# A Fourier mixing and maxout kernel: other load order, full-array transposes and engine orders in batch 0

## Chip, cores, metric

One core of a Trainium2 chip. The metric is device time of one launch in microseconds (us). "Span" is the part of it that the trace covers, some 2 us less. All runs told here are of state fast.

In the views of the profile, PE is TensorE, PEld its weight loads, DVE is VectorE, ACT ScalarE, POOL GpSimd; PEclk is the granted TensorE clock as a share of the full one. A line of the waits view says who waited for whom, then us in total, times, longest us. A timeline line gives start and length in us and ends in the idle time before it and what ended that. A "look" is the traced run of a kernel in a job; a "job" is a set of kernels run in turns on one chip.

## The reference, cut to what matters

```python
X = np.fft.rfft(x, axis=1)                       # x: (8, 3072, 256)
y = np.fft.irfft(X * (filt_r + 1j * filt_i), n=3072, axis=1)
h1 = y @ w1;  h2 = y @ w2                        # 24576 tokens, 256 -> 1024
out = np.maximum(h1, h2) @ w_out                 # -> 256
```

The kernel splits 3072 as 128 x 24 and does the transforms as matmuls. max(h1, h2) is taken as relu(h1 - h2) + h2, so Wd = w1 - w2, and M = w2 @ w_out.

## The kernel before, as far as it matters

Batch 0 is worked off first, in SBUF alone; the others go through DRAM (f1, f2) beside the dense part (s4, moe_h, moe_o), which fills TensorE. In batch 0: S1 (128-point transform), T1 (transposes), s2 (24-point, with the sine table U), pq (product with the filter, which is expanded into F), s3 (inverse, with the tables VP and VQ; ScalarE copies its result to Zt), T2 (transposes), then s4. F_r is the filter's real part as loaded. For the later batches f1 writes ad in DRAM, bt is what is read back of it, and s2 of f2 reads bt.

```python
for c in range(6): load_x(0, c)                  # in front of the iotas, on GpSimd's queue
load_f(0); load_f(1)
G.iota(pid, ...)                                 # five more follow; C1, the cosine table, needs them
...
def first_t1(g, E):                              # 16 transposes of half the array
    for c, i, dh, b in ...:                      # [loops joined]
        TE.transpose(pt[64*b:64*b+64, c, i, 128*dh:128*dh+128], a_[:, 2*(t0+4*c+i) + b], I128)

def first_s2(g, pool):                           # [s2's matmuls into px cut]
    for k in range(2):
        pq.append(pqpool.tile([128, 2, 2, D], BF16, tag="pq", name="pq"))
        E, src = V, px[:, k]
        if k == 1 and pool:                      # one of the two products on GpSimd,
            E = G                                # which needs ScalarE's copy xs
            src = apool.tile([128, 2, D], FP32, tag="at", name="xs")
            S.activation(src[0:FROWS], px[0:FROWS, k], AF.Copy)
        E.tensor_tensor(pq[k][0:FROWS], src..., F[0:FROWS, :, k, 2*g:2*g+2], OP.mult)
...
for n, g in enumerate(order):                    # the product loop, eight groups
    if n < 7: expand_f(order[n + 1], 1, S)       # filter rows to F: 16 matmuls, a ScalarE copy
    if n == 6: fix_f()
    pq = first_s2(g, n in (0, 2, 4))
    if n in (1, 3, 5): prep_wd(n // 2, *wf)      # w2 as bf16, Wd: on GpSimd
    if pend: first_s3(*pend)                     # s3 of the group before
    pend = g, pq
```

## Time and profile before

| | before |
|---|---|
| time | 563.4 us, median of 2 (562.47 to 564.33) |
| first pq / last Zt copied | 34.2 / 61.1 us |
| first s4 / copy of M begins (the first moe_o follows) | 63.0 / 82.8 us |
| from M (start of its copy, here and below) to the end | 478.4 us |

The table follows the chain in time: up to the first pq the filter and U must be ready; to the last Zt runs the product loop; to M the first tiles and the weight preparation; the rest is dense. The lines are in the prediction.

### The profile page before, as it was taken

Reading aid. Unit: us, or ns where it says so; the run is one execution under the profiler, and the core shown is the slowest. Engines: PE = TensorE matmul, PEld = TensorE weight load, DVE = VectorE, ACT = ScalarE, POOL = GpSimd, SP = SyncE. Lnnn points to the kernel's source line nnn. Section 1 sums busy time; section 2 is a strip of 40 time slices with the busy share of each in tenths; the row PEclk is TensorE's granted clock in tenths of the full one; section 3 lists DMA queues with packets and bytes.
Section 4 is the critical chain, followed back from the end, with each engine's and each line's share of the span. In section 5 each row is a group of like instructions: output and inputs, shape, how many; then the busy total and the mean of one; then the engine's idle time right before and its main releaser. Section 6 shows DMA issues by size and latency. Waiting matters only on the chain.

```text
span 561.2 us, 12527 instructions
## 1 busy us (share of the span) xinstructions
PE 513.0 (91%) x5324; PEld 355.3 (63%) x5401; DVE 317.1 (57%) x420; ACT 341.3 (61%) x601; POOL 70.3 (13%) x123
## 2 busy tenths in 40 slices
PE   2866689999999999999999999998999999999992
PEld 2743446666766766667666666676666666677771
DVE  5746414963586357634874387545873578434430
ACT  4576474776578657775677557754776456555440
POOL 7127001101100120011100210012000000000000
PEclk9875689999999999999999999999999999999997
DMA  9950258568967894669856994689566926421111
GB/s 171 282 95 11 49 138 133 129 166 262 181 143 234 212 228 124 189 175 217 191 125 198 214 216 117 200 203 209 127 182 167 196 97 163 123 75 76 67 48 75
DMA packets 67596, 87.07 MB, mean 155 GB/s; under 512 B 3986, under 2 KB 48276, under 8 KB 66452
## 3 DMA queue, kind: packets, MB, share of 16 engines
q1 hardware_dynamic: 51908, 44.31, 36.3%
q0 software_dynamic: 15632, 41.95, 28.2%
q8 instruction: 42, 0.69, 0.5%
q14 instruction: 14, 0.11, 0.1%
HBM read 53.74 MB, written 47.19 MB: 180 GB/s over the span
## 4 chain that ended last, share of the span: by engine, by line
PE 48%; issue 18%; DMA 5%; DVE 2%; POOL 1%; ACT 0%; POOLq 0%; SPq 0%
PE po L527 18%; PE ph L502 16%; PE po L522 4%; DMA bt<-ad 3%; PE pz L372 3%; PE px L391 3%; PE pa L337 2%; PE py L486 2%; DMA ad<-at 2%; DVE pq L396 1%; POOL out_dram L533 1%; ACT at L338 0%; SPq L347 0%; DVE ot L529 0%; DVE gt L505 0%
## 5 line engine op out<-in xcount | busy, mean ns | idle before, releaser
L507 ACT ACTIVATE gt<-ph 128x512 bf16<-128x512 f32 x307 | 182.8, 602 | 114.5 <-PE ph L502 113.6
L527 PE MATMUL po<-Wo,gt 128*128 128x256 bf16 x1536 | 229.8, 273 | 3.2
L527 PEld LDWEIGHTS <-gt 128*128 128x128 bf16 x1536 | 150.3, 98 | 57.5
L396 DVE TENSOR_TENSOR pq<-px,F 120x1024 bf16<-120x1024 f32 x112 | 131.6, 1217 | 24.0 <-PE px L391 23.2
L529 DVE COPY ot<-po 128x512 f32<-128x512 f32 x96 | 66.2, 690 | 110.6 <-PE po L527 110.0
L376 ACT ACTIVATE zt<-pz 112x512 bf16<-112x512 f32 x112 | 60.8, 594 | 45.9 <-PE pz L372 40.6
L502 PEld LDWEIGHTS <-Wd 128*128 128x128 bf16 x768 | 70.3, 98 | 26.2 <-issue 12.4
L533 POOL DMA_DIRECT2D out_dram<-ot x48 | 25.8, 537 | 453.5 <-DVE ot L529 415.3
L505 DVE TENSOR_SCALAR gt<-ph 128x512 bf16<-128x512 f32 x77 | 52.8, 686 | 35.1 <-PE ph L502 27.5
L338 ACT ACTIVATE at<-pa 128x512 bf16<-128x512 f32 x84 | 50.4, 615 | 7.7 <-PE pa L337 6.2
L337 PE MATMUL pa<-xb,C 128*128 128x512 bf16 x83 | 31.2, 383 | 0.6 <-ACT zr L434 0.5
L486 PE MATMUL py<-G,zr 128*128 128x128 bf16 x384 | 30.2, 221 | 1.5 <-DVE zr L432 0.8
L372 PE MATMUL pz<-pq,VP 56*64 56x256 bf16 x448 | 28.7, 271 | 1.0 <-DVE pq L396 0.8
L486 PEld LDWEIGHTS <-zr 128*128 128x128 bf16 x384 | 25.1, 99 | 6.8 <-issue 3.5
L372 PE MATMUL pz<-pq,VQ 56*64 56x256 bf16 x448 | 28.0, 268 | 0.0
L92 POOL DMA_DIRECT2D xb<-in_x_dram x48 | 26.2, 556 | 9.9 <-DMA Fs<-in_filt_i_dram 3.9
L391 PE MATMUL px<-bt,U 48*64 48x256 bf16 x448 | 23.7, 281 | 1.6 <-DMA bt<-ad 1.6
L451 DVE TENSOR_TENSOR pq<-px,F 120x1024 bf16<-120x1024 f32 x13 | 15.2, 1215 | 11.1 <-PE px L441 5.2
L391 PEld LDWEIGHTS <-U 48*64 48x64 bf16 x448 | 8.3, 104 | 13.8 <-issue 11.8
L434 ACT ACTIVATE F<-pf 128x1024 bf16<-128x1024 f32 x16 | 15.5, 1031 | 1.7 <-PE pf L115 1.7
L464 PE MATMUL pz<-VP,pq 56*128 56x48 bf16 x128 | 6.9, 213 | 10.2 <-POOL pq L451 6.1
L372 PEld LDWEIGHTS <-VP 56*64 56x64 bf16 x448 | 13.2, 106 | 3.1 <-DVE pq L396 1.6
(354 smaller groups left out, 562.9 us busy)
## 6 DMA issues: line engine op xcount, KB each, us to landing
out_dram<-ot POOLq DMA_DIRECT2D x48, 512.0 KB, 4.5
xb<-in_x_dram POOLq DMA_DIRECT2D x48, 256.0 KB, 7.3
ad<-at SPq DMA_DIRECT2D x42, 256.0 KB
bt<-ad SPq DMA_DIRECT2D x28, 384.0 KB
zd<-zt SPq DMA_DIRECT2D x56, 192.0 KB
zr<-zd SPq DMA_DIRECT2D x14, 768.0 KB
wf<-in_moe_w_dram POOLq DMA_DIRECT2D x2, 1024.0 KB, 16.5
Fs<-in_filt_r_dram POOLq DMA_DIRECT2D x1, 768.0 KB, 11.6
```

What stands on the lines that cost most here:

```text
L337: TE.matmul(pa, C1, xb[b, c // 2][:, 2 * (c % 2):2 * (c % 2) + 2], start=True, stop=True)
L338: S.activation(at[:, 2 * (c % 2):2 * (c % 2) + 2], pa, AF.Copy)
L372: TE.matmul(pz[c][64 * k:64 * k + 64, i], W[64 * c:64 * c + 56, 2 * g + i, k], pq[k][64 * c:64 * c + 56, ri, i], start=(ri == 0), stop=(ri ...
L376: S.activation(zt[0:ROWS, c, o:o + 2], pz[c][0:ROWS], AF.Copy)
L391: TE.matmul(px[k][64 * c:64 * c + 64, i], U[64 * k:64 * k + 48, t_], bt_[64 * k:64 * k + 48, t_], start=True, stop=True)
L396: V.tensor_tensor(pq[k][0:FROWS], px[k][0:FROWS].rearrange("p (o i) d -> p o i d", o=1).to_broadcast([FROWS, 2, 2, D]), F[0:FROWS, :, k, 2 ...
L486: TE.matmul(py[:, n], zr[b][:, 4 * i + n, 128 * dc:128 * dc + 128], G1, start=True, stop=True)
L502: TE.matmul(ph, Wd[:, dc, 128 * j:128 * j + 128], y_[:, dc].rearrange("p a b -> p (a b)"), start=(dc == 0), stop=(dc == 1))
L505: V.tensor_scalar(gt[tt][:, j], ph, 0.0, None, OP.max)
L507: S.activation(gt[tt][:, j], ph, AF.Relu)
L527: TE.matmul(p_, g_[:, jj, 128 * n:128 * n + 128], Wo[:, jj], start=False, stop=(jj == 7))
L529: V.tensor_copy(ot[tt][:, n - 1:n + 1], po[tt])
```

## The change

The intent is to shorten the stretch in which TensorE isn't the bound: tables at once, ScalarE occupied with the filter while x is still landing, full-array transposes, a product loop that doesn't wait on GpSimd, a warm TensorE, and ScalarE relieved in the first tiles. The core of the diff (cuts marked with ...):

```diff
-    for c in range(6):
-        load_x(0, c)
-    load_f(0)
-    load_f(1)
     pid = init.tile([128, 1], FP32)
 ... iotas ...
+    load_f(0)
+    load_x(0, 0)
+    load_x(0, 1)
 ... Sel, two loads of x0, I128 and SW, two loads ...
+    load_f(1)
-    def spin(n):
-        pd = p2.tile([128, 2, 512], FP32, tag="p2", name="pd")
+    def spin(pd, n):
 ...
-            S.activation(w2T[:, 2 * jp:2 * jp + 2], pt, AF.Copy)
+            V.tensor_copy(w2T[:, 4 * k:4 * k + 4], pt)        # bf16 transposes, in two parts
 ...
-        S.activation(at[:, 2 * (c % 2):2 * (c % 2) + 2], pa, AF.Copy)
+        evac(V if b == 1 and c % 2 else S, at[:, 2 * (c % 2):2 * (c % 2) + 2], pa)
 ...
-                          C1.rearrange("p (k a) -> p a k", a=2), start=True, stop=True)
+                          C1.rearrange("p (t b a) -> p b a t", b=2, a=2), start=True, stop=True)
 ...
-                    for b in range(2):
-                        TE.transpose(pt[64 * b:64 * b + 64, c, i, 128 * dh:128 * dh + 128],
-                                     a_[:, 2 * (t0 + 4 * c + i) + b], I128)
+                    TE.transpose(pt[:, c, i, 128 * dh:128 * dh + 128],
+                                 At[:, 2 * dh:2 * dh + 2].rearrange("p b m t -> p t (b m)")[:, t0 + 4 * c + i], I128)
 ...
+        if pool:
+            xs = apool.tile([128, 2, D], FP32, tag="at", name="xs")
+            S.activation(xs[0:FROWS], px[0:FROWS, 1], AF.Copy)
         pq = []
 ...
         pz = p2.tile([128, 2, 512], FP32, tag="p2", name="pz")
+        spin(pz[:, 0], 2)
 ...
+    order = (1, 0, 2, 3, 4, 5, 6, 7)
+    for e, c in ((3, 0), (1, 1), (0, 2), (1, 3), (0, 4), (0, 5)):
+        for _ in range(e):
+            expand_f(order[len(done)], 0, S)
+            done.append(0)
         first_s1(c)
 ...
     for n, g in enumerate(order):
 ...
-        if n < 7:
-            expand_f(order[n + 1], 1, S)
 ...
-        pq = first_s2(g, n in (0, 2, 4))
+        pend.append(first_s2(g, n in (2, 4, 6)))
 ...
-        if pend:
-            first_s3(*pend)
-        pend = g, pq
-    first_s3(*pend)
 ...
+        if n < 6:
+            expand_f(order[n + 2], 1, S)
+        if n > 1:
+            first_s3(*pend.pop(0))
+    first_s3(*pend.pop(0))
+    first_s3(*pend.pop(0))
 ...
-        plan(j - 1, first_t2, j, (S, V)[j % 2], ps)
-    plan(7, prep_w)
+        plan(j - 1, first_t2, j, V, ps)
+    plan(4, prep_w, 0)
+    plan(5, prep_w, 1)
+    plan(6, prep_w, 2)
-    plan_f2(1, spaced(19, 1.8, 9), 29, 35)
+    plan_f2(1, spaced(18, 1.8, 9), 28, 34)
```

The two matmuls of `spin` write where s3 writes next, and nothing reads them.

More of the change, by code (lines that the diff above doesn't have):

```diff
@@ L72 @@
     xpool = ctx.enter_context(tc.tile_pool(name="xpool", bufs=8))
-    apool = ctx.enter_context(tc.tile_pool(name="apool", bufs=6))
+    apool = ctx.enter_context(tc.tile_pool(name="apool", bufs=5))
     bpool = ctx.enter_context(tc.tile_pool(name="bpool", bufs=2))
@@ L156 @@
            allow_small_or_imprecise_dtypes=True)
+    load_f(0)
+    load_x(0, 0)
+    load_x(0, 1)
     V.memset(I128, 0.0)
+    V.memset(Sel, 0.0)
     V.memset(SW, 0.0)
-    V.memset(Sel, 0.0)
-    V.memset(U.rearrange("p t (q x) -> p t q x", q=2)[:, :, :, 24:32], 0.0)
-    V.memset(VP[:, :, :, 48:64], 0.0)
+    sl = Sel[:, :, 0:24].rearrange("p m (q j) -> p m q j", q=2)
+    for q in range(2):
+        G.affine_select(out=sl[:, :, q], in_=sl[:, :, q], pattern=[[-1, 8], [-8, J]], compare_op=OP.not_equal,
+                        fill=1.0, base=0, channel_multiplier=1)
+    load_x(0, 2)
+    load_x(0, 3)
     G.affine_select(out=I128, in_=I128, pattern=[[-1, 128]], compare_op=OP.not_equal,
@@ L167 @@
                         fill=1.0 - 2.0 * q, base=-12 * (1 - q), channel_multiplier=1)
-    sl = Sel[:, :, 0:24].rearrange("p m (q j) -> p m q j", q=2)
-    for q in range(2):
-        G.affine_select(out=sl[:, :, q], in_=sl[:, :, q], pattern=[[-1, 8], [-8, J]], compare_op=OP.not_equal,
-                        fill=1.0, base=0, channel_multiplier=1)
+    load_x(0, 4)
+    load_x(0, 5)
+    load_f(1)
     def table_c():
@@ L288, in load_w @@
         return w1f[:, 0], w1f[:, 1]
-    def spin(n):
-        pd = p2.tile([128, 2, 512], FP32, tag="p2", name="pd")
+    def spin(pd, n):
         for _ in range(n):
-            TE.matmul(pd[:, 0], SW, VP[:, 0:4].rearrange("p u b n -> p (u b n)"), start=True, stop=True)
+            TE.matmul(pd, SW, VP[:, 0:4].rearrange("p u b n -> p (u b n)"), start=True, stop=True)
     def prep_wd(k, w1f, w2f):
@@ L304, in load_wo, with prep_w @@
         G.dma_start(out=Wo, in_=moe_w_out.rearrange("(c p) j -> p c j", p=128))
-    def prep_w():
-        for jp in range(4):
-            pt = ps.tile([128, 2, D], FP32, tag="ps")
-            for ji in range(2):
+    def prep_w(k):
+        if k < 2:
+            pt = ps.tile([128, 4, D], BF16, tag="ps", name="pt")
+            for ji in range(4):
                 for dc in range(2):
-                    j = 2 * jp + ji
-                    TE.matmul(pt[:, ji, 128 * dc:128 * dc + 128], w2b[:, dc, 128 * j:128 * j + 128],
-                              I128, start=True, stop=True)
-            S.activation(w2T[:, 2 * jp:2 * jp + 2], pt, AF.Copy)
+                    TE.transpose(pt[:, ji, 128 * dc:128 * dc + 128],
+                                 w2b[:, dc, 128 * (4 * k + ji):128 * (4 * k + ji) + 128], I128)
+            V.tensor_copy(w2T[:, 4 * k:4 * k + 4], pt)
+            return
         pm_ = ps.tile([128, 2, D], FP32, tag="ps")
@@ L408, in first_s1 @@
     def first_s1(c):
-        pa = p2.tile([128, 2, 2, 4, 64], FP32, tag="p2", name="pa")
+        pa = p2.tile([128, 2, 2, 2, 4, T], FP32, tag="p2", name="pa")
         for dh in range(2):
             for n in range(4):
-                TE.matmul(pa[:, dh, :, n], xb[0, c][:, n, 128 * dh:128 * dh + 128],
-                          C1.rearrange("p (k a) -> p a k", a=2), start=True, stop=True)
-        S.activation(At[:, :, :, 4 * c:4 * c + 4].rearrange("p h a n k -> p (h a) (n k)"),
-                     pa.rearrange("p h a n k -> p (h a) (n k)"), AF.Copy)
+                TE.matmul(pa[:, dh, :, :, n], xb[0, c][:, n, 128 * dh:128 * dh + 128],
+                          C1.rearrange("p (t b a) -> p b a t", b=2, a=2), start=True, stop=True)
+        S.activation(At[:, :, 0:48].rearrange("p h (a n) t -> p h a (n t)", a=2)[:, :, :, 128 * c:128 * c + 128],
+                     pa.rearrange("p h b a n t -> p (h b) a (n t)"), AF.Copy)
     def first_t1(g, E):
@@ L422, in first_t1 @@
                 for dh in range(2):
-                    a_ = Af[:, 3072 * dh:3072 * dh + 4096].rearrange("p (m k) -> p k m", k=64)
-                    for b in range(2):
-                        TE.transpose(pt[64 * b:64 * b + 64, c, i, 128 * dh:128 * dh + 128],
-                                     a_[:, 2 * (t0 + 4 * c + i) + b], I128)
+                    TE.transpose(pt[:, c, i, 128 * dh:128 * dh + 128],
+                                 At[:, 2 * dh:2 * dh + 2].rearrange("p b m t -> p t (b m)")[:, t0 + 4 * c + i], I128)
         o = bt[0][0:ROWS, 8 * (g // 2):8 * (g // 2) + 8].rearrange("p (c u) d -> p c u d", c=2)[:, :, 2 * (g % 2):2 * (g % 2) + 2]
@@ L445, in first_s2 @@
             pq.append(pqpool.tile([128, 2, 2, D], BF16, tag="pq", name="pq"))
-            E, src = V, px[:, k]
-            if k == 1 and pool:
-                E = G
-                src = apool.tile([128, 2, D], FP32, tag="at", name="xs")
-                S.activation(src[0:FROWS], px[0:FROWS, k], AF.Copy)
+            E, src = (G, xs) if k and pool else (V, px[:, k])
             E.tensor_tensor(pq[k][0:FROWS],
@@ L453, in first_s2 @@
                             F[0:FROWS, :, k, 2 * g:2 * g + 2], OP.mult)
-        return pq
+        return g, pq
     def first_s3(g, pq):
         pz = p2.tile([128, 2, 512], FP32, tag="p2", name="pz")
+        spin(pz[:, 0], 2)
         for dh in range(2):
@@ L543 @@
     Zt = late.tile([128, 2, 128, N2], BF16, name="Zt")
-    Af = init.tile([128, 7168], BF16, name="At")
-    At = Af[:, 0:6144].rearrange("p (h a n k) -> p h a n k", h=2, a=2, n=N2)
-    V.memset(Af[:, 6144:7168], 0.0)
+    At = init.tile([128, 4, 64, T], BF16, name="At")
+    G.memset(At[:, :, 48:64], 0.0)
+    G.memset(U.rearrange("p t (q x) -> p t q x", q=2)[:, :, :, 24:32], 0.0)
+    G.memset(VP[:, :, :, 48:64], 0.0)
     bt[0] = bpool.tile([128, T, D], BF16, tag="bt", name="bt")
     uu, mk = tables_u()
+    done = []
     wf = load_w()
-    for c in range(6):
+    for c in range(4):
         load_x(1, c)
-    load_wo()
-    for c in range(6):
+    order = (1, 0, 2, 3, 4, 5, 6, 7)
[3 more added lines that the diff above has]
+            done.append(0)
         first_s1(c)
     sines_u(uu, mk)
-    order = (4, 5, 6, 7, 2, 3, 1, 0)
     for g in order[:4]:
@@ L559 @@
     tables_pe()
-    for g in order[:4]:
-        expand_f(g, 0, S)
+    expand_f(order[5], 0, S)
+    expand_f(order[0], 1, S)
+    tables_q(0, S)
     for g in order[4:]:
         first_t1(g, V)
+    expand_f(order[1], 1, S)
     tables_q(1, S)
-    tables_q(0, V)
-    for g in order[4:]:
-        expand_f(g, 0, S)
-    pend = None
-    expand_f(4, 1, S)
+    pend = []
     for n, g in enumerate(order):
-        if n < 7:
-            expand_f(order[n + 1], 1, S)
-        if n == 6:
+        if n == 1:
             fix_f()
-        pq = first_s2(g, n in (0, 2, 4))
+        pend.append(first_s2(g, n in (2, 4, 6)))
         if n in (1, 3, 5):
             prep_wd(n // 2, *wf)
-        if pend:
-            first_s3(*pend)
-        pend = g, pq
-    first_s3(*pend)
+        if n == 3:
+            load_x(1, 4)
+            load_x(1, 5)
+            load_wo()
+        if n in (1, 3):
+            expand_f(order[6 + n // 2], 0, S)
+        if n < 6:
[4 more added lines that the diff above has]
+    first_s3(*pend.pop(0))
     zr[0] = zrpool.tile([128, N2, D], BF16, tag="zr", name="zr")
```

## The prediction

> **What bounds the kernel now.** I read the page's slices first (a digit is the busy share in tenths of 14 us), to see where TensorE isn't the bound.
>
> ```profile
> PE   2866689999999999999999999998999999999992
> DVE  5746414963586357634874387545873578434430
> ACT  4576474776578657775677557754776456555440
> PEclk9875689999999999999999999999999999999997
> ```
>
> From slice seven on PE is full and the clock whole. The first six slices, some 84 us, are different: that is batch 0's own chain and the first tiles. The windows view gives the stretches (busy time with instruction counts, then clock, DMA share, GB/s).
>
> ```profile
> 37.00:66.00 29.00, 18.88 (x406) 11.82 (x407) 16.33 (x16) 13.48 (x17) 13.15 (x9) 0.50 0.12 20
> 63.00:82.60 19.60, 16.78 (x115) 10.29 (x118) 3.46 (x5) 14.89 (x28) 0.00 (x0) 0.85 0.30 100
> 252.00:302.00 50.00, 49.20 (x506) 33.69 (x514) 34.54 (x41) 31.73 (x60) 4.81 (x9) 1.00 0.80 188
> ```
>
> At 252 to 302 us PE is 98% busy; the change leaves that part alone. At 37 to 66 us no engine is above 65%, and TensorE runs at half clock: a latency chain. At 63 to 82.6 us ScalarE is busiest (14.9 of 19.6 us) and VectorE nearly idle (3.5).
>
> The timeline dates the milestones (start, length).
>
> ```profile
> 9.20 4.16 PE L412 MATMUL pa<-C,xb 128*128 128x128 bf16 x48 [9.20 <-ACT C L188]
> 23.66 4.21 PE L425 MATMUL pt<-I,At 128*64 128x128 bf16 x64
> 29.45 5.60 ACT L434 ACTIVATE F<-pf 128x1024 bf16<-128x1024 f32 x6
> 34.17 2.35 DVE L451 TENSOR_TENSOR pq<-px,F 120x1024 bf16<-120x1024 f32 x2 [4.06 <-ACT F L434]
> 62.99 1.03 PE L486 MATMUL py<-G,zr 128*128 128x128 bf16 x8 [0.79 <-DVE zr L432]
> 82.84 0.69 DVE L320 CAST M<-pm__1424 128x512 bf16<-128x512 f32 x1 [8.10 <-PE pm__1424 L318]
> ```
>
> S1 could not start before the cosine table (9.2), the products pq begin at 34.2, after ScalarE has expanded the filter, the first s4 is at 63.0 and step 8 (the first moe_o) at 82.6. In the waits of the first 64 us, the product loop shows what it waits for:
>
> ```profile
> ACT Zt L469 <- PE pz L464: 9.5, 6, 2.8
> PE pz L464 <- POOL pq L451: 6.1, 3, 2.6
> PE pz L464 <- DVE pq L451: 4.1, 5, 1.1
> ```
>
> s3 stands in order right behind the next s2, so every GpSimd product (2.12 us) holds TensorE.
>
> **What the Trainium skill says.** (1) "TensorE: Matmul & The Clock Gate", section "Weight-path perf modes": fast weight load needs all 128 weights, not fp32, in one column step; "TensorEngine Tiling (Array Packing)", "Feature Incompatibilities", excludes it under column tiling. The trace agrees: 64 loads of 64 columns took 4.08 us, 64 ns each, though half as wide, while eight 128-column pairs of s4 take 0.45 us in the chain, 56 ns each. (2) The same clock page, Part 1: an idle window of about 3.4 us halves the clock, a busy one restores it. The trace shows the half clock from 37 to 66 us with waits of at most 2.7 us, so a thin load is enough here. (3) "VectorE: DVE Perf Modes", "Why PSUM operands drop a tier": 2-byte PSUM reads may still run double rate, fp32 ones not. The trace agrees: 1024 bf16 from PSUM in 0.69 us, 512 fp32 in 0.69 us.
>
> **The change, part by part.**
>
> *Loads and tables.* In front of GpSimd's six first x0 loads (1.25 to 4.5 us) there were no iotas; now the six iotas go first (spaced some 0.14 us, 0.85 in all) and then F_r. So pid is there at about 1.0 instead of 5.7, and the table C1 at about 4.4 instead of 9.15 (2.9 us after, as now). F_r is issued near 1.7. Bytes moved by 7.5 us before were 0.95 MB, which is F_r (0.79) plus the SP loads (0.16); with 0.45 us of later start and a tail of engines running apart, I estimate F_r at 8.7. x0 landed before from 5.4 (weights of S1) to about 12.6 (the wait on that load's lane is over by 13.0), 1.44 us apart; behind F_r that becomes 10.0 to 17.
>
> *ScalarE until S1 ends.* Work after F_r: five expansions of 1.02 and six S1 evacuations of 0.935 (5.61/6) = 10.7 us, hence 9.3 to 20.0. Before, S1 ended at 15.85: 4.2 us later, but five expansions (5.1 us) are done, which before were only beginning at 21.8. The sines (2.46 us; their arguments are ready at about 13) end at 22.5 instead of 20.45.
>
> *Transposes.* 128 half-array transposes become 64 full ones. At 56 ns 32 of them are 1.8 us instead of 4.2; at half clock (128/1.2 = 107 ns by the page) 3.4. VectorE's 0.69 us per group of eight becomes the bound: 4 x 0.7 = 2.8 against 4.2, twice. First four done 23.7, VP copy (0.96) 24.7, the other four 28.4. ScalarE meanwhile: three expansions and two VQ copies (1.02 each) from 24 to 30.3. The first s2 can run at 28.8 and pq begins at **29.3 instead of 34.2: 4.9 us**.
>
> *The product loop.* VectorE: 13 products x 1.225 = 15.9, plus fix_f 2 x 0.34 + 0.48 = 1.2, so 17.1 us. ScalarE: eight expansions 8.2, eight Zt 6.5, three xs 1.8 = 16.5. GpSimd: 3 x 2.12, Wd 2 x 2.36, three loads 2 = 13 (the w2b casts are done before). TensorE per group: s2 to s3 0.57, s3 to expansion 0.75, expansion to s2 0.98 in the present timeline at half clock, 2.3 in all; the two unread products add 2 x 0.43 there, 3.2 per group and 25 in all; at full clock about 1.8 + 0.43 + a drain = 2.4, 19 in all. At half clock TensorE would have no gap, which should bring its clock up, so I take 2.4. s3 now lags two groups, so GpSimd's product has some 4.8 us to come in. Walking the eight groups in order with the four PSUM buffers (an expansion waits for the s2 tile four allocations back) costs about 2 us of VectorE gaps; pq ends at 50.3, the last two s3 and Zt at 52.4, T2 and its copy at 54.0, **s4 at 54.2 instead of 63.0: 8.8 us**. The loop itself is thus 24.9 instead of 28.8 us.
>
> *First tiles.* ScalarE loses two T2 copies (2.2), six of twelve f1 copies (3.6) and four w2T copies (2.3), and keeps f1 3.6, gt 8 x 0.6, y 1.2 = 9.6 us. VectorE now has five T2 copies 3.45, six f1 4.15, y 1.4, w2T 1.4, M 0.7 = 11.1. TensorE at full clock: ph 16 x 0.216 = 3.5, T2 40 x 0.056 = 2.2, f1 12 x 0.216 = 2.6, s4 0.45, weights 16 x 0.056 + 16 x 0.108 = 2.6: 11.4. Step by step I get 1.4 us for steps 0 to 3, 2.1 and 1.4 for the next two, 4 for the last two with M's wait: 13 us instead of the present 18.2 (64.4 to 82.6). The pure weight stage (79 to 82.8, partly at half clock) vanishes among the steps. **Gain 5.2**; the lost half clock at 80 to 83 is part of it.
>
> *Unchanged.* 478.6 us follow step 8. f2(1) begins one step earlier: its rows must land by then. Before, the read was issued at 79.8, DMA fell quiet near 90.3, and s2 came at 95.4. After, the read starts near 66.5, lands near 77, and step 18 is near 80: no wait, with 3 us of slack. One attention buffer fewer: the sixth f1 tile reuses one written some 8 us before; no wait.
>
> Sum: 4.9 + 3.9 (loop) + 5.2 = 14.0; 563.4 - 14.0 = **549.4**, put at **549.5**.
>
> **Rivals.** (a) *F_r first only moves the wait.* x0 lands 4.4 us later and S1 ends 4.2 later; if F_r lands at 11 instead of 8.7, everything behind it slides 2.3 us: 552. For it: DMA is full to 35 us (share above 0.9). Against: ScalarE, not DMA, is the bound behind F_r. (b) *The unread products become the bound.* If the clock stays at half, the loop takes 25 + 3 us and the first tile starts cold: the loop's gain and 1 us more are lost, 554. For it: half clock for 29 us at 65% busy. Against: TensorE would be gapless. (c) *The gain of the first tiles is given back* at step 18, if ad, bt and x loads land late: up to 5 us, 554.5. For it: DMA sits at 1.2 from 82 to 90. Against: the slack above. (d) *It goes better:* clock full all along, VectorE never waits (loop 21 us), first tiles at 11.5: 544.
>
> **Range and chances.** Rivals a to c cost 2.5 to 5 us each and are unlikely together; d gives 5.5. So 543.5 to 556. Faster by over 2% means below 552.1: one of a, b, c would spoil it, each at some one in ten: 0.73. Within 2%: 0.26. Slower would need a new stall of over 25 us, of which nothing shows: 0.01.
>
> **What would show it.** Right: C1 done near 4.4; first expansion before S1, near 9; S1's last evacuation near 20; transposes as 64 of 128*128, VectorE copies back to back; pq from 29; clock near 1.0 from 30 on; s4 at 54; step 8 near 67.5; no PE wait on bt at step 18; the rest 478 to 479 us long. Wrong: half clock in the loop, s3 still waiting on GpSimd, PE waiting for bt<-ad near 80, or a first s4 after 57.

## The result, and the profile after

545.36 us, median of 2 (544.98 to 545.74). Ratios here are the mean time of one kernel's fast runs over that of the other's of the same rounds, so not quite the ratio of the medians quoted. The ratio to before is 0.968 (95% interval 0.9605 to 0.9755). Ten more runs of the same kernel in later jobs took 545.8 to 550.6 us, with ratios 0.9698 (0.9652 to 0.9744) and 0.9727 (0.9702 to 0.9752). So the gain is some 15 to 18 us, and the first two runs were at its upper end.

The busy slices of the page of the changed kernel (13.6 us each):

```profile
PE   3886999999999999999999999999999999999992
DVE  8595759634882476438773677438763788344331
ACT  4794637774787568855675567745775565554540
PEclk9798999999999999999999999999999999999997
```

PE is full from slice five instead of seven, and the long dip of the clock (slices three to five before) is gone. The milestones in the timeline of the changed kernel (start, length):

```profile
2.77 1.00 ACT L190 ACTIVATE C<-uc,zero 128x32 bf16<-128x32 f32 x4 [0.76 <-DVE uc L186]
8.56 2.75 PE L115 MATMUL pf<-Fs,Sel 96*32 96x256 bf16 x48 [8.56 <-DMA Fs<-in_filt_r_dram]
16.90 2.94 ACT L414 ACTIVATE At<-pa 128x1024 bf16<-128x1024 f32 x3
19.99 3.61 PE L423 MATMUL pt<-I,At 128*128 128x128 bf16 x32 [1.73 <-ACT At L414]
26.55 2.32 PE L423 MATMUL pt<-I,At 128*128 128x128 bf16 x32
30.43 2.36 DVE L448 TENSOR_TENSOR pq<-px,F 120x1024 bf16<-120x1024 f32 x2 [0.70 <-PE px L439]
52.08 1.03 PE L484 MATMUL py<-G,zr 128*128 128x128 bf16 x8 [0.79 <-DVE zr L430]
66.45 0.69 DVE L321 CAST M<-pm__1363 128x512 bf16<-128x512 f32 x1 [1.13 <-PE pm__1363 L319]
```

First pq 3.7 us earlier, first s4 10.9, M 16.4; from M to the end 477.5 us against 478.4. The windows view of the two kernels, each over its own product loop (PE, PEld, DVE, ACT and POOL busy, then clock, DMA share, GB/s); before:

```profile
34.00:61.00 27.00, 15.82 (x392) 9.36 (x391) 17.77 (x16) 14.87 (x19) 14.04 (x9) 0.53 0.16 25
```

and after:

```profile
30.00:49.00 19.00, 14.89 (x446) 9.04 (x453) 15.84 (x16) 15.66 (x20) 14.03 (x10) 1.00 0.42 60
```

VectorE and ScalarE are busy over 80% of the loop instead of 66 and 55%: they, far more than the waits between the engines, now set its pace. The waits of the changed kernel up to 54 us say the same, against the 9.5 and 6.1 us of before:

```profile
ACT Zt L467 <- PE pz L462: 3.2, 4, 2.2
PE pz L462 <- POOL pq L448: 1.8, 1, 1.8
DVE pq L448 <- ACT xs L443: 1.0, 2, 0.5
```

### The profile page after: what moved, and what is told of

It is laid out like the page before. It is cut to its first block, busy times and chain, and to the rows that moved or that the text cites. A ratio compares the mean times of both kernels' runs of the same rounds, so it can differ in the third digit from the quotient of the medians.

```text
span 544.0 us, 12421 instructions
## 1 busy us (share of the span) xinstructions
PE 507.7 (93%) x5268; PEld 352.8 (65%) x5353; DVE 323.7 (60%) x426; ACT 336.0 (62%) x590; POOL 72.9 (13%) x126
## 3 DMA queue, kind: packets, MB, share of 16 engines
q0 software_dynamic: 15632, 41.95, 29.4%
## 4 chain that ended last, share of the span: by engine, by line
issue 48%; PE 24%; POOL 4%; DVE 0%; POOLq 0%
PE po L525 9%; PE ph L500 8%; POOL out_dram L531 3%; PE po L520 2%; PE pz L372 1%; POOL xb L92 1%; PE px L391 1%; PE pa L337 1%; PE py L484 1%; DVE pq L396 0%; POOLq L690 0%; POOLq L531 0%; POOLq L92 0%
## 5 line engine op out<-in xcount | busy, mean ns | idle before, releaser
L432 ACT ACTIVATE at<-pa 128x512 bf16<-128x512 f32 x78 | 46.8, 600 | 9.4 <-PE pa L337 7.6
L372 PE MATMUL pz<-pq,VP 56*64 56x256 bf16 x448 | 28.8, 271 | 1.6 <-DVE pq L396 1.6
L115 PE MATMUL pf<-Fs,Sel 96*32 96x256 bf16 x256 | 11.0, 312 | 9.2 <-DMA Fs<-in_filt_r_dram 8.6
L391 PEld LDWEIGHTS <-U 48*64 48x64 bf16 x448 | 8.4, 104 | 12.9 <-issue 11.8
L448 DVE TENSOR_TENSOR pq<-px,F 120x1024 bf16<-120x1024 f32 x13 | 15.1, 1214 | 1.7 <-ACT xs L443 1.0
## 6 DMA issues: line engine op xcount, KB each, us to landing
wf<-in_moe_w_dram POOLq DMA_DIRECT2D x2, 1024.0 KB, 14.2
```

The lines of the kernel that those rows point to most:

```text
L372: TE.matmul(pz[c][64 * k:64 * k + 64, i], W[64 * c:64 * c + 56, 2 * g + i, k], pq[k][64 * c:64 * c + 56, ri, i], start=(ri == 0), stop=(ri ...
L391: TE.matmul(px[k][64 * c:64 * c + 64, i], U[64 * k:64 * k + 48, t_], bt_[64 * k:64 * k + 48, t_], start=True, stop=True)
L432: S.activation(out_, in_, AF.Copy)
```

## The experiments

Milestones come from one trace each. "Loop" is from the first pq to the end of the last Zt copy; "tiles" from the first s4 to M; "rest" from M to the end.

| kernel | first pq | loop | tiles | rest | time, us | ratio to before |
|---|---|---|---|---|---|---|
| before | 34.2 | 26.9 | 19.9 | 478.4 | 563.4 | 1 |
| changed | 30.4 | 19.7 | 14.4 | 477.5 | 545.4 | 0.968 |
| no unread products | 29.4 | 19.6 | 15.1 | 478.5 | 547.5 | 0.9708 |
| s3 lags one group | 29.7 | 21.2 | 14.9 | 479.1 | 548.5 | 0.9724 |
| xs late | 29.7 | 24.5 | 12.9 | 478.9 | 549.3 | 0.9751 |
| half transposes | 32.4 | 20.3 | 15.1 | 478.6 | 550.0 | 0.9748 |
| changed, second job | 28.6 | 20.6 | 14.6 | 481.3 | 548.1 | 0.9698 |
| x0 ahead of F_r | 32.5 | 19.8 | 14.1 | 477.7 | 551.3 | 0.9757 |
| old loop | 29.6 | 23.8 | 13.9 | 479.0 | 550.7 | 0.9757 |
| before + new tiles | 34.4 | 26.9 | 14.2 | 478.8 | 558.5 | 0.9891 |
| changed, third job | 29.9 | 20.5 | 14.8 | 481.6 | 547.3 | 0.9727 |
| f2 later | 29.8 | 19.8 | 14.0 | 476.2 | 544.2 | 0.9665 |
| gaps filled, f2 later | 29.5 | 19.9 | 12.9 | 476.2 | 542.1 | 0.963 |
| before + new loop | 35.6 | 19.9 | 19.5 | 478.8 | 556.9 | 0.9891 |

Lines of one job share the runs of before: four after "changed", four from "changed, second job", four from "changed, third job". The rest scatters by 4 us between three looks at one and the same kernel.

How far can a loop time be trusted? The three looks at the changed kernel have 19.7, 20.6 and 20.5 us, but from the first pq to the end of the last product (VectorE's or GpSimd's) 17.3 us each; they differ only behind it, where the clock from 46 to 48 us is 1.00 in the first look and 0.50 in the second. So this shorter stretch stands beside the loop below where the argument rests on it.

Totals were expected against the 545.4 us of the first two runs. The same kernel took 547.3 and 548.1 us in the later jobs, and the first job had no run of it, so the totals of that job's four edits settle little.

### No unread products

```diff
         pz = p2.tile([128, 2, 512], FP32, tag="p2", name="pz")
-        spin(pz[:, 0], 2)
```

> The changed kernel without the sixteen unread products. Theory A (the lag of two groups carries the loop): the loop, from the first pq to the last Zt, stays at 20 to 22.5 us (19.7 in the changed kernel, 26.9 before), total within 1 us of the changed kernel's (545.4). Theory B (the unread products carry it by keeping the clock up): the clock in the loop falls to 0.5 as before, the loop goes to 24 us or more, total 549 to 551.

The loop took 19.6 us, as with them (17.3 to the last product, as with them), although the clock fell. The total, 547.5 us, is 1.1 us above what theory A allowed. Windows view of this kernel:

```profile
30.00:49.00 19.00, 12.73 (x424) 9.12 (x416) 15.26 (x16) 15.35 (x20) 14.00 (x10) 0.76 0.46 63
```

So the unread products do lift the clock (1.00 with them) but do not carry the loop; theory B falls. The clock here is 0.76 in the mean, not the 0.5 that theory B had. The tiles after the loop took 15.1 us against 14.4 to 14.8 in the looks at the changed kernel; that is hardly more than such looks differ among themselves, so a gain there isn't shown.

### s3 one group behind

```diff
-        if n > 1:
+        if n > 0:
             first_s3(*pend.pop(0))
     first_s3(*pend.pop(0))
-    first_s3(*pend.pop(0))
```

> The changed kernel with s3 one group behind s2, as before. Theory A: TensorE waits for each of the three GpSimd products again, 1 to 2 us each, the loop grows by 3 to 5 us, total 548.5 to 550.5. Theory B: the unread products are there, so the loop grows by at most 1 us and the total stays under 546.5.

The loop grew by 1.5 us against the first look (to the last product by 1.8: 19.1 against 17.3), between the 3 to 5 of theory A and the 1 of theory B; that the total, 548.5 us, meets theory A is chance. In the waits from 29 to 56 us of this kernel TensorE waits on GpSimd hardly more than in the changed kernel (1.8); it is VectorE's wait for xs that grew, from 1.0 us:

```profile
DVE pq L448 <- ACT xs L443: 3.2, 2, 1.9
...
PE pz L462 <- POOL pq L448: 2.2, 2, 1.3
```

The second group of lag thus matters less than I had it, and by another way than a wait on GpSimd.

### xs behind VectorE's first product

```diff
-        if pool:
-            xs = apool.tile([128, 2, D], FP32, tag="at", name="xs")
-            S.activation(xs[0:FROWS], px[0:FROWS, 1], AF.Copy)
 ...
+            if k == 1 and pool:
+                E = G
+                src = apool.tile([128, 2, D], FP32, tag="at", name="xs")
+                S.activation(src[0:FROWS], px[0:FROWS, k], AF.Copy)
```

> The changed kernel with ScalarE's copy xs issued behind VectorE's first product again, so GpSimd starts each of its three products about 1.2 us later. If the lag of two hides GpSimd, only the last of the three shows, where s3 already waited 1.9 us: total plus 0.5 to 1.3 us (546 to 546.7). If the place of xs carries the gain of the loop: plus 3 us or more (548.5 and over).

The loop grew by 4.8 us (to the last product by 4.9: 22.1 against 17.3): of the two orders of issue, the place of xs is the larger. The wait of TensorE on GpSimd is not how it comes about. In the waits of this kernel from 29 to 56 us:

```profile
ACT xs L448 <- DVE pq L449: 5.1, 3, 2.9
...
DVE pq L449 <- ACT F L432: 2.6, 1, 2.6
```

xs and VectorE's product read the same PSUM tile px, and the program runs its two readers one after the other. Issued second, xs waits until VectorE has worked off its backlog; in this trace ScalarE starts nothing else during that wait (2.9 us before the xs at 36.3), so the expansions of F behind xs are late too, and then VectorE waits for F. Issued first, xs costs VectorE 0.5 us at a time. In the kernel before, the same wait stood in the view of the first 64 us, and I had passed over it:

```profile
ACT xs L450 <- DVE pq L451: 2.1, 3, 0.9
```

### Half-array transposes

The edit puts the old bodies of S1 and T1, and the old layout of At, back into the changed kernel:

```diff
 ... S1 as before ...
-                    TE.transpose(pt[:, c, i, 128 * dh:128 * dh + 128],
-                                 At[:, 2 * dh:2 * dh + 2].rearrange("p b m t -> p t (b m)")[:, t0 + 4 * c + i], I128)
+                    a_ = Af[:, 3072 * dh:3072 * dh + 4096].rearrange("p (m k) -> p k m", k=64)
+                    for b in range(2):
+                        TE.transpose(pt[64 * b:64 * b + 64, c, i, 128 * dh:128 * dh + 128],
+                                     a_[:, 2 * (t0 + 4 * c + i) + b], I128)
 ... the layout of At as before ...
```

> The changed kernel with the old S1 layout and 128 transposes of half the array. If TensorE bounds the transposes: 4.2 us for each four groups instead of 3.4 (at half clock) and 2.3, the first pq 2 to 2.7 us later than 30.4, total 547.2 to 548.2. If ScalarE's and VectorE's copies bound that stretch (rival): first pq less than 0.8 us later, total under 546.3.

First pq at 32.4 us, 2.0 behind the first look and 2.7 to 3.0 behind the three kernels of the same job (29.4 to 29.7); M at 69.7; the total, 550.0 us, is above the expected. The timeline of this kernel:

```profile
19.87 4.17 PE L425 MATMUL pt<-I,At 128*64 128x128 bf16 x64 [1.77 <-ACT At L414]
26.45 4.39 PE L425 MATMUL pt<-I,At 128*64 128x128 bf16 x64
```

The three others of the job took 3.0 to 3.4 us for the first four groups and 2.2 to 2.4 for the last four. TensorE did bound the transposes, and the copies don't hide the difference.

### The changed kernel again

> The changed kernel again, so that others of this job can be held against it on one chip. Both theories: ratio to before 0.967 to 0.970; first pq at 29.4 to 30.5 (it varied so between the kernels run so far, with the point where TensorE's clock comes back), loop of 19.7 us from the first pq to the last Zt.

Ratio 0.9698, first pq at 28.6, earlier than expected; the loop, 20.6 us, longer at its end as told above. In this look the clock stayed whole in the first transposes. Windows view, this look:

```profile
20.00:25.00 5.00, 4.49 (x133) 3.92 (x135) 3.37 (x5) 3.81 (x8) 0.00 (x0) 1.00 1.03 386
```

and the first look at the same kernel:

```profile
20.00:25.00 5.00, 5.00 (x105) 4.67 (x109) 3.03 (x5) 2.45 (x5) 0.00 (x0) 0.50 1.03 385
```

One and the same program meets the half clock there or doesn't; it goes with 1.8 us of the first pq.

### x0 ahead of F_r

```diff
-    load_f(0)
     load_x(0, 0)
     load_x(0, 1)
 ...
     load_x(0, 5)
+    load_f(0)
     load_f(1)
 ...
-    for e, c in ((3, 0), (1, 1), (0, 2), (1, 3), (0, 4), (0, 5)):
+    for e, c in ((0, 0), (0, 1), (0, 2), (0, 3), (0, 4), (0, 5)):
 ...
+    for _ in range(5):
+        expand_f(order[len(done)], 0, S)
+        done.append(0)
     sines_u(uu, mk)
```

> The changed kernel with its iotas first, but the six x0 loads in front of F_r and the five early expansions behind S1. Theory: F_r first fills ScalarE's empty time; with x0 first, S1's last evacuation comes at 13 to 15 us instead of 19.8, then ScalarE waits for F_r until about 16.5, five expansions and the sines end near 24.5 instead of 22.2, first pq 1.5 to 2.5 us later, total plus 1.5 to 2.5. Rival: what counts is that the iotas went ahead of the loads, whichever load is first: first pq within 0.7 us, total within 0.8 us.

First pq 32.5 us, 2.1 to 3.9 later than in the looks at the changed kernel (the theory had 1.5 to 2.5), total 3.2 us more than the changed kernel of its job; the direction is the theory's, the size larger, because F_r landed at 18.2 and not by 16.5. The timeline of this kernel shows S1's last copy at 15.5, then ScalarE idle until F_r is there:

```profile
15.50 1.02 ACT L414 ACTIVATE At<-pa 128x1024 bf16<-128x1024 f32 x1 [0.48 <-PE pa L412]
19.25 4.69 ACT L432 ACTIVATE F<-pf 128x1024 bf16<-128x1024 f32 x5 [2.73 <-PE pf L115]
```

Part of this edit is that the sines, which the program has behind the expansions, now wait for F_r too (end 26.3 instead of 22.2), so it tests the order of loads together with the order of work that goes with it.

### The old loop in the changed kernel

The edit joins those of the first three experiments.

> The changed kernel with all three features of the old product loop: no unread products, s3 one group behind, xs behind VectorE's first product. Singly they cost the loop 0, 1.4 and 4.8 us. If they add up: loop of 25 to 26.5 us, total plus 5.5 to 7 against the changed kernel of this job. If the lag of two was what made the late xs costly (ScalarE's wait for VectorE being longer there), the sum is smaller: loop of 22 to 24 us, total plus 3 to 4.5.

Loop 23.8 us (21.4 to the last product): they don't add up. The total is 2.6 us more than the changed kernel of the job, a little under the 3 to 4.5 expected. As a table of the loop, us:

| | xs late | xs first |
|---|---|---|
| lag one | 23.8 (no unread products) | 21.2 |
| lag two | 24.5 | 19.7 |

The lag of two gains 1.5 us with xs first; with xs late it gains nothing. This isn't the whole loop of before, which took 26.9 us: the changed kernel also expands F two groups ahead, behind s2, takes the groups in another order and gives other products to GpSimd. What of the 3.1 us each of these is worth was not tested; the experiment with the new loop in the kernel before shows that none of them is needed once xs is first and the lag two.

### The first tiles alone, in the kernel before

```diff
-        S.activation(at[:, 2 * (c % 2):2 * (c % 2) + 2], pa, AF.Copy)
+        evac(V if b == 1 and c % 2 else S, at[:, 2 * (c % 2):2 * (c % 2) + 2], pa)
 ... prep_w in three parts with bf16 transposes and VectorE copies ...
-        plan(j - 1, first_t2, j, (S, V)[j % 2], ps)
-    plan(7, prep_w)
-    plan_f2(1, spaced(19, 1.8, 9), 29, 35)
+        plan(j - 1, first_t2, j, V, ps)
+    plan(4, prep_w, 0)
+    plan(5, prep_w, 1)
+    plan(6, prep_w, 2)
+    plan_f2(1, spaced(18, 1.8, 9), 28, 34)
```

> The kernel before with only the change to the first tiles: T2 copies and half of batch 1's f1 copies on VectorE, the weight preparation as bf16 transposes spread over steps 4 to 6, batch 1's f2 one step earlier. Theory: the gain of that stretch stands by itself: from the first s4 to M 14 to 14.6 us instead of 19.9, total 5 to 6 us less than before. Rival: it was the warm clock or the earlier loads that shortened the stretch: 16.5 us or more, total at most 3.5 less.

Tiles 14.2 us instead of 19.9, time 5.8 us less than before (medians of the job). The part stands by itself. ScalarE's relief is to be seen in the windows view of this kernel, from its first s4 to M:

```profile
63.20:77.50 14.30, 13.58 (x114) 9.89 (x117) 9.65 (x16) 8.78 (x15) 0.00 (x0) 0.86 0.27 101
```

PE 95% busy, against 86% in the prediction's line of 63 to 82.6 us before; VectorE 9.7 us (3.5 before), ScalarE 8.8 (14.9).

### The product loop alone, in the kernel before

```diff
+        if pool:
+            xs = apool.tile([128, 2, D], FP32, tag="at", name="xs")
+            S.activation(xs[0:FROWS], px[0:FROWS, 1], AF.Copy)
 ...
-        if pend:
-            first_s3(*pend)
-        pend = g, pq
-    first_s3(*pend)
+        if n > 1:
+            first_s3(*pend.pop(0))
+    first_s3(*pend.pop(0))
+    first_s3(*pend.pop(0))
```

> The kernel before with only the lag of two groups and xs ahead of VectorE's first product, without unread products. Theory: these two carry the loop: 26.9 us becomes 20.5 to 22.5 us although TensorE's clock stays at half for most of it, total 4.5 to 6.5 us less than before. Rival: the new loop needs the full clock or the other order of expansions too: 24 us or more, total at most 3 us less.

Loop 19.9 us; the first pq waits 1.4 us longer, as xs now stands before it on ScalarE, so the last Zt comes 5.6 us earlier; time 6.1 us less (medians). This at half clock, without unread products. Windows view:

```profile
40.00:45.00 5.00, 5.00 (x132) 3.01 (x130) 3.98 (x5) 4.46 (x6) 5.00 (x3) 0.50 0.01 3
45.00:50.00 5.00, 4.12 (x122) 2.58 (x116) 5.00 (x6) 3.71 (x5) 4.65 (x4) 0.50 0.09 7
```

Two small edits to the order of issue make the loop; neither the full clock nor the new order of expansions is needed for it. (To the last product it is 18.3 us, 1 us more than in the changed kernel.)

### A third look, f2 later, and an attempt at a better version

> The changed kernel once more, as the measure for the two next runs on the same chip: ratio to before 0.967 to 0.971. First pq 28.6 us where TensorE's clock is whole in the first transposes, 29.4 to 30.5 where it is halved; PE's wait on bt<-ad after 66 us between 0.8 and 3 us, as it fell in the two looks so far.

> The changed kernel with f2 of batches 5 to 7 two steps (some 2.5 us) later. If PE's waits on bt<-ad in the main part are what differs from run to run there: no such wait of over 0.3 us, the part from M to the end at 477 us or less in each look, total 0.5 to 2.5 us less than the changed kernel of this job and its runs closer together. If the wait moves to the later z reads instead, or the run-to-run difference has another source: no difference.

```diff
-        plan_f2(n, spaced(196 + o, 3.5, 9), 215 + o, 225 + o)
+        plan_f2(n, spaced(198 + o, 3.5, 9), 217 + o, 227 + o)
```

In the third look the rest took 481.6 us and PE waited for batch reads in the main part (waits of PE from 66 us on):

```profile
PE px L391 <- DMA bt<-ad: 3.2, 2, 1.9
```

in the first look 477.5 us with

```profile
PE px L391 <- DMA bt<-ad: 0.8, 1, 0.8
```

With f2 two steps later the view has no such line, the rest is 476.2 us, and the four runs lie between 543.5 and 545.0 where the six of the changed kernel lie between 546.2 and 550.6. So the wait explains 3.2 of the 5.4 us between the third look and f2 later, and the edit removes it. The gain, 3.1 us, is more than the 0.5 to 2.5 expected, as the changed kernel of this job waited longer than in the looks before (ratio 0.9727 where 0.967 to 0.971 was expected). Most of the other 2.2 us is in the clock. In the third look it is halved for some 3.5 us just behind the longer of the two waits (1.9 us, over at 370.3), while PE is busy throughout; windows view of the third look:

```profile
371.50:375.00 3.50, 3.49 (x14) 1.97 (x14) 2.78 (x4) 0.74 (x2) 0.00 (x0) 0.54 1.06 232
```

At a clock of 0.54, 3.5 us lose about 1.6 us; that is an estimate from this line. The second look has the same behind a wait of 1.8 us (0.52 from 370 to 373.4 us); the first look, with one of 0.8 us, has 1.00 there. Some 0.6 us stay open.

> An attempt at a better version: f2 later as in f4, eight unread products between S1 and the transposes, four before T2 and four before the first s4, one early copy of F on VectorE, and the second Wd product of GpSimd behind its last pq. Expected from the traces: whole clock in the first transposes and the first tile, first pq 28 to 28.8 us, loop 18.3 to 19.2 us, first s4 to M 13.2 to 14 us; total 2.5 to 5 us less than the changed kernel of this job. If the unread products do nothing for the clock there: first pq stays at 29.4 or later.

```diff
-            expand_f(order[len(done)], 0, S)
+            expand_f(order[len(done)], 0, V if c == 3 else S)
 ... the last first_s1 ...
+    pd = p2.tile([128, 2, 512], FP32, tag="p2", name="pd")
+    for _ in range(8):
+        TE.matmul(pd[:, 0], C1, xb[0, 5][:, 0:2], start=True, stop=True)
 ...
-        if n in (1, 3, 5):
-            prep_wd(n // 2, *wf)
+        if n in (1, 3, 6):
+            prep_wd(n // 2 if n < 6 else 2, *wf)
 ...
+    pd = p2.tile([128, 2, 512], FP32, tag="p2", name="pd")
+    spin(pd[:, 0], 4)
     zr[0] = zrpool.tile([128, N2, D], BF16, tag="zr", name="zr")
     first_t2(0, V, p2)
+    spin(pd[:, 1], 4)
 ... f2 later, as above ...
```

542.1 us, ratio 0.963: the fastest of all, 5.2 us below the changed kernel of its job, of which the later f2 gives 3.1 (544.2). The rest of what I planned came in part. The clock is whole or nearly so in the first transposes and in front of the first tile, where "f2 later" has 0.66 and 0.50 (in the transposes the second look was whole without unread products too, so one trace doesn't prove them the cause there). Windows view of this kernel:

```profile
20.00:25.00 5.00, 5.00 (x135) 3.95 (x133) 3.14 (x5) 3.68 (x7) 0.00 (x0) 1.00 1.03 388
...
50.00:55.00 5.00, 4.29 (x33) 2.83 (x33) 1.67 (x3) 1.26 (x3) 0.00 (x0) 0.86 0.39 72
```

and the tiles shrank to 12.9 us. But the first s4 comes 0.8 us later than with f2 later alone, at 52.3, so M comes only 0.4 us earlier, and the two traced runs differ by 0.4 us. The kernel is 2.1 us faster than "f2 later" in the medians; where the rest of that comes from, the traces don't show. And the first pq came at 29.5, not 28 to 28.8: the early copy on VectorE held a PSUM buffer that S1 needed, as this kernel's timeline shows, and S1's last copy began at 19.6:

```profile
18.52 1.09 PE L412 MATMUL pa<-C,xb 128*128 128x128 bf16 x8 [0.86 <-DVE F L430]
```

The loop stayed at 19.9 us: in the last group but one TensorE still stands for 1.7 us, although GpSimd's product is done by then; the trace names no releaser, and I leave it open.

## Why the prediction was right, point by point

The time fell in the range (543.5 to 556), 4.1 us below the 549.5 named; over all twelve runs of the changed kernel the median is 547.2. Its three terms, 4.9 (first pq), 3.9 (from there to the first s4) and 5.2 us (from there to M), measured 3.7, 7.2 and 5.5: the sum came close because one fell short and one went over.

| step | predicted | first look |
|---|---|---|
| C1 | 4.4 | 3.8 |
| F_r there | 8.7 | 8.6 (the first expansion's matmuls begin) |
| S1's last copy ends | 20.0 | 19.8 |
| first four groups of transposes | 2.8 us | 3.6 us, at half clock |
| copies of the last four groups | 2.8 us | 2.5 us, back to back |
| first pq | 29.3 | 30.4 (28.6 to 30.4 in three looks) |
| VectorE's last pq ends | 50.3 | 47.3 |
| first s4 | 54.2 | 52.1 |
| M earlier by | 14.0 | 16.4 |
| rest | 478 to 479 | 477.5 (to 481.6) |

*Up to S1's end*: right in each term, and shown by the experiment with x0 first; rival (a) did not come. *Transposes*: right that half-array ones would cost TensorE time; wrong that VectorE's 0.69 us copies would bound the first four groups, since the clock was half there in that look: 3.6 us instead of 2.8 are most of the 1.1 us. Where the clock was whole (second look), the first pq came at 28.6, before the 29.3 named. The 1.8 us that I had for 32 full-array transposes at full clock were too few: the last four groups took 2.3 us in the first look.

*The product loop* is the term that was mis-sized: 21.0 us from the first pq to the end of the last (29.3 to 50.3) against 16.8 (30.4 to 47.3). I had VectorE's work at 17.1 us and then added waits from a walk with 2.4 us of TensorE per group; the last five groups' s2 came 2.5, 2.3, 2.0 and 1.5 us apart, VectorE was busy for 15.8 us, and its waits for xs named above sum to 1.0 us. Two reasons in it were wrong, though the sum was on the safe side. I gave the credit to the lag of two; it is worth 1.5 us, and xs's place, which I did not name at all, up to 4.8. And I made the full clock a condition (rival b): without unread products the loop runs as fast. The rival's own case, unread products at half clock, never occurred and is untested.

*First tiles*: 19.9 to 14.4, a gain of 5.5 where 5.2 was said, and shown alone in the kernel before. Rival (c) did not come: no PE wait on batch 1's rows at step 18 (the only wait on bt in the first look is at 367 us).

*Unchanged part*: it is not quite constant. Its wait on batch reads varies from run to run; that I had not seen, and the first two runs were lucky by a microsecond or two.

The parts add up: first tiles alone 5.8 us, loop alone 6.1, and the first pq 3.7 to 5.5 us earlier, 15.6 to 17.4 together, against 15.4 to 18.0 from the three ratios.

## What to carry to other kernels

Where two engines read one PSUM tile and the program orders them, let the engine with the short job read first: here ScalarE, waiting for VectorE's backlog, held up everything that the program had behind that wait. Load first what an engine could otherwise work on only late, even if the "main" data then lands later, provided that engine is the next bound. Before keeping TensorE warm by spare products, ask whether it is the bound there: in the loop they changed the clock and not the time; in front of the first tile a gain beyond 0.4 us isn't shown. And where a wait for a read is cut, look at the clock behind it too: here a wait of 1.9 us was followed by about 1.6 us more at half clock.

## What the Trainium skill lacked or had wrong

- "TensorE: Matmul & The Clock Gate", Part 1, gives full clock after some 3.4 us of sustained activity. In the kernel before with the new loop, PE counts as busy for all of 40 to 45 us and the clock stays at 0.50. The profile's busy time is thus no measure of what the clock gate counts. The page itself says in Part 4 that transposes don't count the same way; in the first look PE was busy for all of 20 to 25 us, mostly with transposes, at 0.50, in the second the same work ran at 1.00, so the runs do not settle that.
- "GPSIMD Engine Reference", Specifications, names the SBUF interfaces that GpSimd shares with VectorE, and "SBUF — State Buffer" has one engine blocked for a whole instruction of the other. No page has a wait over a row of instructions. In the changed kernel two VectorE instructions on 12 elements each ended only when GpSimd's loads and memsets were through, 4.5 us after the first began, though the longest single one of GpSimd's took 1.83 us; the same two took 0.23 us each before. The timeline of the changed kernel:

```profile
5.54 4.51 DVE L222 TENSOR_SCALAR kb<-kb,col 128x12 f32<-128x12 f32 x1
...
7.25 1.83 POOL L543 MEMSET At<- 128x2048 bf16 x1
```

  It cost nothing there, as the sines waited for ScalarE until 19.6. That a shared interface is the cause is argued from the times, not tested.
- No page has the spread of DMA reads that a tuned schedule sits on: PE's wait for one kind of read was 0.8, 2.8 and 3.2 us in three looks at one program.
